# The opening of a windowed attention and SwiGLU kernel: one cast on another engine, gate matmuls among the attention's last products, the first projection begun on two chunks

## The chip, the cores and the metric

The kernel runs on one core of one Trainium2 chip. The metric is the device time of one launch in microseconds, taken as a median over runs. One execution was also taken by the hardware profiler; all starts and durations below come from it. The engines are called PE (TensorE), DVE (VectorE), ACT (ScalarE), POOL (GpSimd) and SP (SyncE). Each runs its own instructions in order, and they wait for each other by semaphores. Loads are issued from SP, ACT and POOL and are carried out by 16 DMA engines.

## The reference

There are 8 batches of 8 heads, 576 positions and 64 elements per head. Attention is causal with a window of 64 positions. The result, laid out as 4608 tokens by 512, goes through a gated block with 1536 hidden columns:

```
scores = (q @ k^T) / 8,  kept where 0 <= i - j < 64
attn   = exp(scores - max);  attn = attn / (sum(attn) + 1e-9)
x      = (attn @ v) as [4608, 512]
g      = x @ w_gate;  h = g * sigmoid(g) * (x @ w_val)
out    = h @ w_out
```

Inputs and output are float32. The kernel multiplies in bf16.

## The kernel before

**Tiles.** The 4608 tokens are nine tiles of 512. Tile t, up to the seventh, holds the first 512 positions of batch t; one later tile, called LAST, gathers the last 64 positions of all batches. The eight heads go in four pairs, u = 0 to 3. The model dimension has four chunks of 128 (one for each pair), the hidden dimension twelve blocks of 128.

**Stages of a tile.** `scores(t, u)` makes the products of one pair in a two-bank PSUM tile (tag "a", two buffers), and ACT takes their exponential into a tile E; from tile 1 on DVE multiplies by the mask. `totals` sums E by a matmul with ones; ACT takes the logarithm and then `invert` its negative exponential, so that r is the inverse sum. `mix` multiplies E by the values, and `scale` (DVE) multiplies by r and writes chunk u of xT. `values` is `mix` and then `scale`. `v2` is a copy of the values shifted by 64 rows, written by `shift_pair` on DVE. Then for each hidden block m, `gate_value(t, m)` runs four matmuls with wg and four with wv over the chunks of xT into two PSUM banks (tags "g" and "v" of pool `ps_f`, two buffers each); `gate_end` takes Silu on ACT and multiplies on DVE into block m of hT. `gate_part` does the matmuls of one chunk c for several blocks. Last, `project_part` multiplies hT with wo over the twelve blocks, into `ps_f` banks as well, and the output goes out through SP.

**Order.** The schedule is manual: each engine executes its instructions in the order in which the program writes them. In steady state, tile t's gate blocks are followed by tile t+1's scores and tile t's projection, interleaved by hand.

**The opening.** Tile 0's queries and keys come in float32 by SP and ACT queues, a pair at a time. `cast_first(u, i)` makes bf16 of them, with i = 0 for queries and 1 for keys. The table `casts` says on which engine. `turn_pe(u)` transposes both on PE, and ACT or DVE copies them out of PSUM. POOL then issues, on one queue, half of tile 0's values, the weights wg and wv in slices of columns, tile 1's raw keys `raw_k`, the last weight slice, tile 1's queries (`load_qk(1)`, four loads into q_s), and wo with tile 1's values among it:

```
    weights_gv(1280, 1536)
    load_qk(1)
    weights_o(0, 4)
    weights_o(4, 8)
    load_v(nc.gpsimd, v1[1], 1)
    weights_o(8, 12)
```

Loads issued by POOL use eight semaphores in turn, so each waits until the load eight places earlier has landed. `keep_warm` is a matmul into an unused bank.

During tile 0's gate blocks, ACT casts the raw keys of tile 1 in blocks 5 to 8 and PE transposes them in blocks 6 to 9. From block 9 on, `turn_q(1, u)` transposes tile 1's queries on DVE, one behind each block's hT. It needs all four loads of q_s. After block 11 come `scores(1, u)` and `columns(c0, c1)`, which is tile 0's projection for all four 128-row parts over blocks c0 to c1; the four banks it accumulates in are taken in the order g, v, g, v. They are the banks of gate blocks 10 and 11.

The lines of the profile that matter: L73 loads of q and k by runs, L87 q_s, L128 values, L166 wg and wv, L172 wo, L180 transposes on PE, L192 `turn_q`, L233 scores, L239 their exponential, L241 mask, L251 totals, L259 and L262 logarithm and inverse, L275 `mix`, L285 `scale`, L312 `gate_part`, L325 and L326 `gate_end`, L332 `gate_value`, L341 `project_part`, L450 casts.

Of the kernel before, what the change touches and what calls it, by code (L numbers as in the profile page):

```python
# [17 lines left out]
def kernel(  # L18
# [42 lines left out]
    def batch(t):  # L61
        return t if t < LAST else t - 1
# [51 lines left out]
    def load_qk(t):  # L114
        q_s = load_q(t)
        if t == 1:
            staged[t] = q_s, None
            return
        if t == LAST:
            groups = [(b, S - P) for b in range(4)]  # L120
        else:
            groups = [(batch(t), P * g) for g in range(4)]
        k_s = stage.tile([P, 4, 4, 4 * D], BF16, name="k_s", tag="k")
        staged[t] = q_s, load_k(k_s, groups)

    def load_v(eng, dst, t, which=range(4)):
        for i in which:
            eng.dma_start(  # L128
                dst[:, i], v[batch(t), :, P * i:P * i + P].rearrange("h r d -> r h d")
            )  # L130
# [19 lines left out]
    def shift_pair(t, u):  # L150
        hs = slice(2 * u, 2 * u + 2)
        a, b = v1[t % 2][:, :, hs], v2[t % 2][:, :, hs]
        nc.vector.tensor_copy(b[64:128, 1:4], a[64:128, 0:3])
        nc.vector.tensor_copy(b[0:64], a[0:64])
# [16 lines left out]
    def weights_o(c0, c1):  # L171
        nc.gpsimd.dma_start(  # L172
            wo[:, c0:c1, :],
            moe_w_out[P * c0:P * c1].rearrange("(c r) f -> r c f", r=P),
        )
# [73 lines left out]
    def totals(t, u, d_ps):  # L249
        for h in range(2):  # L250
            nc.tensor.matmul(  # L251
                d_ps[64 * h:64 * h + 64], ones[:, 0:D], weights[t, u][:, h, :]
            )

    def room(n):
        return fsb.tile([P, 2, 512], FP32, name="r", tag="r", bufs=4)[:, 0:n]

    def log(r, d_ps):
        nc.scalar.activation(r, d_ps, AF.Ln)  # L259

    def invert(r):
        nc.scalar.activation(r, r, AF.Exp, scale=-1.0)  # L262
# [8 lines left out]
    def mix(t, u, o_ps):  # L271
        E = weights.pop((t, u))
        for m in range(8):
            for h in range(2):
                nc.tensor.matmul(  # L275
                    blocks(o_ps[64 * h:64 * h + 64], t, m, m + 1),
                    (v1, v2)[m // 4][t % 2][:, m % 4, 2 * u + h, :] if t == LAST
                    else (v2, v1)[m % 2][t % 2][:, m // 2, 2 * u + h, :],
                    blocks(E[:, h, :], t, m, m + 1),
                )  # L280

    def scale(t, u, o_ps):
        if u == 0:
            xT[t] = att.tile([P, 4, 512], BF16, name="xT", tag="xT")
        nc.vector.tensor_mul(xT[t][:, u, :], o_ps, inverse.pop((t, u)))  # L285

    def values(t, u, o_ps):
        mix(t, u, o_ps)
        scale(t, u, o_ps)
# [12 lines left out]
    def mix_all(t):  # L302
        tiles = wide("ao_ps"), wide("ao_ps")
        for u in range(4):
            mix(t, u, tiles[u // 2][:, u % 2])
        for u in range(4):
            scale(t, u, tiles[u // 2][:, u % 2])

    def gate_part(t, ms, tiles, c):
        for m, pair in zip(ms, tiles):  # L310
            for ps, w in zip(pair, (wg, wv)):
                nc.tensor.matmul(  # L312
                    ps[:], w[:, c, P * m:P * m + P], xT[t][:, c, :],
                    start=(c == 0), stop=(c == 3),
                )

    def gate_tiles():
        return [ps_f.tile([P, 512], FP32, name=x + "_ps", tag=x) for x in "gv"]
# [19 lines left out]
    def project_part(t, ss, tiles, cs):  # L338
        for c in cs:
            for s, o_ps in zip(ss, tiles):  # L340
                nc.tensor.matmul(  # L341
                    o_ps[:], hT[t][:, c, P * s:P * s + P], wo[:, c, :],
                    start=(c == 0), stop=(c == 11),
                )
# [64 lines left out]
    def keep_warm(n):  # L409
        for _ in range(n):  # L410
            nc.tensor.matmul(warm[0:D], ones[:, 0:D], ones[:])
# [32 lines left out]
    on_v, on_p, on_a = nc.vector.tensor_copy, nc.gpsimd.tensor_copy, nc.scalar.copy  # L444
# [4 lines left out]
    def join(copy, dst, src):  # L449
        copy(dst.rearrange("r e (h d) -> r h e d", h=2), src)  # L450

    def one(name):
        return ps_a.tile([P, 2, 512], FP32, name=name, tag="a")[:, 0]

    casts = ((on_a, on_v), (on_p, on_a), (on_a, on_p), (on_v, on_a))

    def cast_first(u, i):
        join(casts[u][i], first[:, i, u], raw[i][:, 2 * u:2 * u + 2])

    def turn_pe(u):  # L460
        tps = [ps_f.tile([P, 512], BF16, name="tp", tag=x) for x in "gv"]
        for i in range(2):
            transposes(tps[i], first[:, i, u])
        (on_v if u else on_a)(queries[0][:, u, :], tps[0][:])
        split_k(kT[0][:, u, :], tps[1][:])
# [3 lines left out]
    turn_pe(0)  # L469
    cast_first(1, 0)  # L470
    cast_first(1, 1)
    load_v(nc.gpsimd, v1[0], 0, (2, 3))
    keep_warm(1)
    scores(0, 0)
    turn_pe(1)
    cast_first(2, 0)
    cast_first(2, 1)
    keep_warm(2)
    scores(0, 1)
# [12 lines left out]
        load_runs(nc.gpsimd, raw_k[:, hs], k, 1, hs)  # L492
    weights_gv(1280, 1536)
    load_qk(1)
    weights_o(0, 4)
    weights_o(4, 8)
    load_v(nc.gpsimd, v1[1], 1)
    weights_o(8, 12)
# [11 lines left out]
    def log_of(u):  # L510
        d_ps = one("d_ps")
        totals(0, u, d_ps)
        inverse[0, u] = room(1)[:, 0]
        log(inverse[0, u], d_ps)
# [6 lines left out]
        values(0, u, ps_f.tile([P, 512], FP32, name="ao_ps", tag="gv"[u])[:])  # L521
    for u in (2, 3):
        shift_pair(0, u)
    log_of(3)
    for u in (2, 3):
        invert(inverse[0, u])
    keep_warm(1)
    pairs = [gate_tiles() for _ in range(2)]
    for c in range(2):
        gate_part(0, (0, 1), pairs, c)  # L530
    for u in (2, 3):
        values(0, u, one("ao_ps"))
    for c in range(2, 4):
        gate_part(0, (0, 1), pairs, c)
    set_silu()
    for m in range(12):
# [11 lines left out]
        if 5 <= m < 9:  # L548
            u = m - 5
            join(on_a, keys[:, u], raw_k[:, 2 * u:2 * u + 2])  # L550
        if 6 <= m < 10:
            u = m - 6
# [10 lines left out]
    def columns(c0, c1):  # L563
        project_part(0, range(4), tiles, range(c0, c1))

    for u in range(4):
        scores(1, u)
        if u == 1:
            columns(0, 4)
    columns(4, 7)  # L570
    for u in (0, 2):
        d_ps, r = wide("d_ps"), room(2)
        for i in range(2):
# [5 lines left out]
    load_v(nc.gpsimd, v1[0], 2)  # L579
    for u in range(4):  # L580
        shift_pair(1, u)
    columns(7, 10)
    mix_all(1)
    columns(10, 12)
    for s in range(4):
# [75 lines left out]
```

## Time and profile before

| What | us |
|---|---|
| median of 6 runs (332.97 to 333.56) | 333.29 |
| the profiled execution's own time | 336.23 |
| its span, first to last instruction | 334.4 |
| PE busy | 321.9 (96%) |
| DVE busy | 210.9 (63%) |
| ACT busy | 168.7 (50%) |
| POOL busy | 139.3 (42%) |
| DMA, mean over the span | 130 GB/s |

The span is that of the profiled execution; 1.83 us of its own time lie around it. Busy shares are means over the span. The opening, tile 0 with tile 1's attention, ends at about 56 us. Inside it POOL's queue of loads is active all the time, and after it PE is busy for 272.2 of 278 us. A wait in the profile is idle time of an engine just before an instruction, with what released it. The granted clock of PE is full in every slice.

### The profile page before, as it was taken

How to read it: one execution, taken by the hardware profiler on the slowest of the kernel's cores; microseconds unless marked ns; L12 is line 12 of the kernel's file. 1: busy time of each engine (PE TensorE's matmuls, PEld its weight loads, DVE VectorE, ACT ScalarE, POOL GpSimd, SP SyncE). 2: the span in 40 equal slices, each digit the busy share in tenths (PEclk: the TensorE clock that was granted, in tenths of full speed). 3: DMA queues.
4: the chain of work that ended last, by engine and by line, in shares of the span. 5: the costliest groups of instructions: out<-in, count | busy, mean ns of one | idle time of the engine just before them, and what ended most of it. 6: DMA issues, size and time to landing. Idle time of an engine off the chain costs nothing.

```text
span 334.4 us, 6954 instructions
## 1 busy us (share of the span) xinstructions
PE 321.9 (96%) x2700; PEld 154.3 (46%) x2743; DVE 210.9 (63%) x325; ACT 168.7 (50%) x239; POOL 139.3 (42%) x249
## 2 busy tenths in 40 slices
PE   8899899999999999999999999999999999999995
PEld 4444344444544454445444544445444544454443
DVE  5855565587557756785669566956786576754431
ACT  5854547337533773367435653465348533853310
POOL 4944434865837993656123996164200000000000
PEclk9999999999999999999999999999999999999999
DMA  7999999999999969939941999199501320020013
GB/s 250 195 192 200 202 190 173 150 169 213 176 223 212 108 108 243 192 51 217 181 94 18 160 196 165 10 186 177 119 1 33 88 63 2 17 79 32 2 33 94
DMA packets 83249, 43.59 MB, mean 130 GB/s; under 512 B 63888, under 2 KB 77968, under 8 KB 83216
## 3 DMA queue, kind: packets, MB, share of 16 engines
q0 software_dynamic: 50416, 23.08, 56.2%
q1 hardware_dynamic: 31776, 19.02, 21.1%
q10 hardware_dynamic: 1024, 1.05, 1.1%
q8 instruction: 21, 0.34, 0.4%
q14 instruction: 12, 0.10, 0.1%
HBM read 54.00 MB, written 9.44 MB: 190 GB/s over the span
## 4 chain that ended last, share of the span: by engine, by line
PE 83%; DMA 12%; POOL 3%; issue 1%; SPq 0%; DVE 0%; POOLq 0%
PE o_ps L341 25%; PE g_ps L332 25%; PE v_ps L332 24%; DMA wo<-in_moe_w_out_dram 4%; DMA wv<-in_moe_w_val_dram 4%; DMA q_s<-in_q_dram 3%; PE s_ps L233 3%; PE ao_ps L275 2%; PE d_ps L251 2%; DMA q_f<-in_q_dram 1%; POOL wg L166 1%; POOL wv L166 1%; PE o_ps L377 1%; POOL v L128 1%; POOL qk_b L450 0%
## 5 line engine op out<-in xcount | busy, mean ns | idle before, releaser
L325 ACT ACTIVATE sg<-g_ps 128x512 f32<-128x512 f32 x108 | 64.4, 597 | 116.4 <-PE g_ps L332 87.7
L326 DVE TENSOR_TENSOR hT<-sg,v_ps 128x512 bf16<-128x512 f32 x108 | 74.7, 692 | 61.1 <-PE v_ps L332 49.8
L332 PE MATMUL g_ps<-xT,wg 128*128 128x512 bf16 x415 | 108.2, 379 | 0.9
L332 PE MATMUL v_ps<-xT,wv 128*128 128x512 bf16 x415 | 107.2, 379 | 0.1
L341 PE MATMUL o_ps<-wo,hT 128*128 128x512 bf16 x396 | 93.5, 380 | 1.8 <-DMA wo<-in_moe_w_out_dram 0.4
L107 POOL DMA_DIRECT2D k_s<-in_k_dram x112 | 60.4, 546 | 35.7 <-DMA q_s<-in_q_dram 21.3
L332 PEld LDWEIGHTS <-wv 128*128 128x128 bf16 x424 | 41.5, 98 | 50.0
L332 PEld LDWEIGHTS <-wg 128*128 128x128 bf16 x424 | 41.3, 98 | 49.5 <-issue 0.6
L341 PEld LDWEIGHTS <-hT 128*128 128x128 bf16 x420 | 39.0, 98 | 48.4 <-issue 4.0
L239 ACT ACTIVATE E<-s_ps 128x1024 bf16<-128x1024 f32 x36 | 35.2, 1020 | 9.3 <-PE s_ps L233 9.3
L202 DVE STREAM_TRANSPOSE kT<-k_s 128x512 bf16<-128x512 bf16 x28 | 35.9, 1281 | 0.0
L259 ACT ACTIVATE r<-d_ps 128x512 f32<-128x512 f32 (+1 forms) x33 | 20.8, 629 | 16.8 <-PE d_ps L251 16.7
L285 DVE TENSOR_TENSOR xT<-ao_ps,r 128x512 bf16<-128x512 f32 x36 | 22.4, 683 | 7.3 <-PE ao_ps L275 7.0
L241 DVE TENSOR_TENSOR E<-E,mask 128x1024 bf16<-128x1024 bf16 x28 | 19.5, 698 | 12.0 <-ACT E L239 12.0
L87 POOL DMA_DIRECT2D q_s<-in_q_dram x28 | 15.2, 553 | 23.2 <-DVE qT L192 13.3
L192 DVE STREAM_TRANSPOSE qT<-q_s 128x512 bf16<-128x512 bf16 x32 | 22.4, 703 | 2.3 <-DMA q_s<-in_q_dram 2.3
L262 ACT ACTIVATE r<-r 128x512 f32<-128x512 f32 (+1 forms) x33 | 22.0, 669 | 1.0
L148 POOL CAST v<-v_f 128x512 bf16<-128x512 f32 x20 | 11.9, 615 | 18.5 <-DMA v_f<-in_v_dram 13.1
L233 PE MATMUL s_ps<-qT,kT 64*64 64x128 bf16 (+1 forms) x640 | 12.4, 211 | 0.2
L387 ACT ACT_TABLE_LOAD x9 | 11.5, 1283 | 2.0 <-issue 1.9
L94 POOL DMA_DIRECT2D q_s<-in_q_dram x16 | 8.6, 629 | 9.2 <-DVE qT L192 9.2
L251 PE MATMUL d_ps<-E,ones 128*64 128x512 bf16 x72 | 11.4, 390 | 0.8 <-ACT E L239 0.8
(102 smaller groups left out, 185.8 us busy)
## 6 DMA issues: line engine op xcount, KB each, us to landing
q_s<-in_q_dram POOLq DMA_DIRECT2D x28, 248.0 KB, 6.8
k_s<-in_k_dram POOLq DMA_DIRECT2D x112, 56.0 KB, 4.9
v_f<-in_v_dram SPq DMA_DIRECT2D x22, 256.0 KB
v<-in_v_dram POOLq DMA_DIRECT2D x18, 128.0 KB, 4.9
wo<-in_moe_w_out_dram POOLq DMA_DIRECT2D x3, 512.0 KB, 12.6
v<-v SPq DMA_DIRECT2D x6, 256.0 KB
v<-v SPq DMA_DIRECT2D x6, 192.0 KB
q_f<-in_q_dram SPq DMA_DIRECT2D x4, 256.0 KB
```

The source lines that it names most:

```text
L107: nc.gpsimd.dma_start(k_s[p0:p0 + 32, g, :, 0:w], k[b, a:H:2, s:s + P].rearrange("u (r e) d -> r u (e d)", e=4) [:, :, 32 * c:32 * c + w],)
L192: nc.vector.transpose(queries[t][:, u, :].rearrange("r (e x) -> r e x", e=16), staged[t][0][:, u].rearrange("r (e d) -> r e d", d=D)[:, :, ...
L202: nc.vector.transpose(dst[:, u, :].rearrange("r (g x e) -> r g e x", g=4, e=4), k_s[:, :, u].rearrange("r g (e d) -> r g e d", d=D)[:, :, ...
L233: nc.tensor.matmul(blocks(s_ps[64 * c:64 * c + 64, h], t, lo, hi), zero[r] if src is None else src[r, u, x:x + 64], blocks(qT[r], t, lo, h ...
L239: nc.scalar.activation(E[:], s_ps[:], AF.Exp, scale=0.125)
L259: nc.scalar.activation(r, d_ps, AF.Ln)
L262: nc.scalar.activation(r, r, AF.Exp, scale=-1.0)
L285: nc.vector.tensor_mul(xT[t][:, u, :], o_ps, inverse.pop((t, u)))
L325: nc.scalar.activation(sg[:], g_ps[:], AF.Silu)
L326: nc.vector.tensor_mul(hT[t][:, m, :], sg[:], v_ps[:])
L332: nc.tensor.matmul(ps[:], w[:, c, P * m:P * m + P], xT[t][:, c, :], start=(c == 0), stop=(c == 3),)
L341: nc.tensor.matmul(o_ps[:], hT[t][:, c, P * s:P * s + P], wo[:, c, :], start=(c == 0), stop=(c == 11),)
```

## The change

Three edits, all in the opening, none in what is computed.

1. The cast of pair 2's queries moves from ACT to POOL and stands ahead of POOL's two value loads; the cast of pair 2's keys moves from POOL to ACT.
2. The gate matmuls of blocks 0 and 1 over chunks 0 and 1 are placed around the values of pairs 2 and 3: chunk 0, pair 2's values, chunk 1, pair 3's values, then chunks 2 and 3. The four gate banks are taken from the pool before `log_of(3)`, and one `keep_warm(1)` goes.
3. The first load of wo, of four blocks, becomes two loads of two blocks. Tile 0's projection begins with blocks 0 and 1, ahead of `scores(1, 0)`; the later groups of blocks are cut at 2, 5 and 8 instead of 4, 7 and 10 (the cut at 10 stays).

```diff
-    casts = ((on_a, on_v), (on_p, on_a), (on_a, on_p), (on_v, on_a))
+    casts = ((on_a, on_v), (on_p, on_a), (on_p, on_a), (on_v, on_a))
...
     cast_first(1, 1)
+    cast_first(2, 0)
     load_v(nc.gpsimd, v1[0], 0, (2, 3))
     keep_warm(1)
     scores(0, 0)
     turn_pe(1)
-    cast_first(2, 0)
     cast_first(2, 1)
...
     load_qk(1)
-    weights_o(0, 4)
+    weights_o(0, 2)
+    weights_o(2, 4)
     weights_o(4, 8)
...
+    pairs = [gate_tiles() for _ in range(2)]
     log_of(3)
     for u in (2, 3):
         invert(inverse[0, u])
-    keep_warm(1)
-    pairs = [gate_tiles() for _ in range(2)]
     for c in range(2):
         gate_part(0, (0, 1), pairs, c)
-    for u in (2, 3):
-        values(0, u, one("ao_ps"))
+        values(0, c + 2, one("ao_ps"))
     for c in range(2, 4):
         gate_part(0, (0, 1), pairs, c)
...
+    columns(0, 2)
     for u in range(4):
         scores(1, u)
         if u == 1:
-            columns(0, 4)
-    columns(4, 7)
+            columns(2, 5)
+    columns(5, 8)
...
     for u in range(4):
         shift_pair(1, u)
-    columns(7, 10)
+    columns(8, 10)
     mix_all(1)
     columns(10, 12)
```

## The prediction, made before the changed kernel had run

> **What bounds the kernel now.** I read the page's busy shares first: PE (TensorE) is busy 321.9 of 334.4 us. By stretches of time, 272.2 of 278 us are busy after 56 us, and about 49.7 of 56 before. So half of PE's idle time, some 6.3 us, lies in the opening, and only the opening is edited. Then the chain that ended last, in order of time (start, length, what):
>
> ```profile
> 8.57 0.83 POOL qk_b L450
> 9.40 0.65 POOL wg L166
> ...
> 15.81 12.10 DMA wv<-in_moe_w_val_dram
> ...
> 28.19 10.43 DMA q_s<-in_q_dram
> ```
> ```profile
> 38.62 12.57 DMA wo<-in_moe_w_out_dram
> 51.20 0.04 issue
> 51.24 1.89 PE o_ps L341 x8
> ```
>
> The reader is to see that from 15.81 to 51.24 us the chain holds no engine: one load follows another, and PE takes over at 51.24. These loads are the one GpSimd queue (q0). Each waits for the landing of the load eight places before it, so eight are under way at any time. By windows the DMA moves 201 GB/s from 19 to 28 us and 193 from 40 to 52. Third, what PE waited for in 0 to 56 us (total, times, longest), and the timeline where it waits:
>
> ```profile
> PE s_ps L233 <- DVE qT L192: 1.6, 2, 0.8
> PE g_ps L312 <- DVE xT L285: 0.6, 1, 0.6
> PE tp L180 <- POOL qk_b L450: 0.5, 1, 0.5
> PE o_ps L341 <- DMA wo<-in_moe_w_out_dram: 0.4, 1, 0.4
> PE tp L180 <- ACT k_b L450: 0.3, 1, 0.3
> ```
> ```profile
> 29.27 0.62 ACT L450 COPY k_b<-k_r 128x512 bf16<-128x512 bf16 x1 [1.58 <-DMA k_r<-in_k_dram]
> 39.67 0.71 DVE L192 STREAM_TRANSPOSE qT<-q_s 128x512 bf16<-128x512 bf16 x1 [2.30 <-DMA q_s<-in_q_dram]
> 40.30 0.65 DVE L326 TENSOR_TENSOR hT<-sg,v_ps 128x512 bf16<-128x512 f32 x1
> 41.49 0.65 DVE L326 TENSOR_TENSOR hT<-sg,v_ps 128x512 bf16<-128x512 f32 x1
> 51.24 1.89 PE L341 MATMUL o_ps<-wo,hT 128*128 128x512 bf16 x8 [0.39 <-DMA wo<-in_moe_w_out_dram]
> ```
>
> The first three waits are what the three edits remove. The last two, and DVE's wait for q_s at 39.67, are arrivals: landings set where PE stands at 29.95 (the transposes of the next keys, after ACT's cast at 29.27), at 40.4 and at 51.24.
>
> **What the Trainium skill says.** "DMA: Bandwidth & Descriptors", section on queues, rings and completion order, has each DMA engine take a ring's descriptors in order. The trace agrees: landings follow the issue order, about 1.3 us apart for 256 KB. "SBUF — State Buffer", section on the two separate sides, says that VectorE and GpSimd share a port pair under an exclusive lock. The trace fits: the GpSimd cast alone took 0.61 us, the one at 8.56 us, beside a VectorE cast, 0.845. "TensorE: Matmul & The Clock Gate", Part 1, says that an idle window of some 3.4 us lowers the clock. The trace grants 1.00 in every slice, and no wait I expect is over 1.3 us, so the dropped warming matmul costs no clock.
>
> **The change part by part.**
>
> *Casts of pair 2.* POOL now casts the queries (0.61 us, 0.845 as the upper bound) ahead of its two value loads, and ACT the keys (0.61) where it cast the queries; the two counts stay. ACT is in the same place (7.74 us). On PE the second four transposes lose their 0.46 us wait; VectorE's copy of the keys then follows its copy of the queries at 9.47 instead of 9.89, so scores of pair 2 and ACT's next exponentials come 0.4 earlier. On POOL's queue stand behind the cast the two value loads (1.87 us) and all weight loads. The cast can start at 6.70, if the third quarter of q is in. The trace doesn't show that landing: quarter 1 was in at 5.96, quarter 3 at about 8.4, and ACT took quarter 2 at 7.74 without a wait. Between, 6.8 is my estimate (256 KB at the window's 360 GB/s take 0.7 us); 7.74 is the late end. Then 6.85 + 0.61 + 1.87 = 9.3 against 9.36 for the first weight load: nothing. The late end gives 10.2 to 10.5, 0.9 to 1.1 us late; the early end 9.2, a gain of 0.2. The value loads go out 0.7 later (landing 12.4 and 13.4, after 11.7 and 12.7); shift_pair at 12.67, then values, can lose about 0.7, under the same cover as the next part.
>
> *Gate parts among sums and products.* Same instructions less one warming matmul (0.22 us). Now the eight matmuls of chunks 0 and 1 run around the values of pairs 2 and 3, so scaling pair 2 overlaps chunk 1. The last gate chunks began at 18.93 after a 0.60 us wait; with 0.4 from the casts, 0.22 from the warming matmul and 0.6 from the wait, PE is some 1.1 us ahead at 20 us (0.9 to 1.3; 0.3 if the values are late). What is late next: wv for columns 768 to 1279 lands at about 28.1 by POOL's waits, and block 6 needed it at 28.41. PE, 1.1 early, would wait 0.85 there. Then the key transposes, at 29.95 behind the landing of k_r, where PE waited 0.3 and now waits to the same 29.95. Gain kept: 0. If that cover were gone, it would be 1.1.
>
> *wo in two loads and two chunks first.* One more POOL issue (0.75 us, POOL idles between waits there), and every later load waits for a landing one place earlier; the last wo load is issued at 39.65 + instead of 38.62, but some 1.3 MB (three parts of wo and four of v) stand ahead of it in the queue, so its landing stays at 51.24. SP's queue carries nothing here that the change touches.
>
> columns(0, 2), eight matmuls of 0.22, move ahead of scores(1, 0), which PE could start at 40.43. They need four PSUM banks. Two of them are the value banks of blocks 10 and 11, which VectorE frees with hT at 40.30 + 0.65 = 40.95 and 41.49 + 0.65 = 42.14, behind the transposes that waited for q_s; the order of instructions shows both waits on DVE. They also need the first half of wo. The whole 512 KB was in by 41.98, so half is in at about 41.98 − 1.2 = 40.8. PE ends block 11 at 39.65, idles 1.15, runs three matmuls with a 0.1 wait, idles to 42.2: 2.55 − 0.65 = 1.9 us of idle time against 0.79 + 0.77 = 1.56 before. PE is thus 0.34 later when it has done chunks 0 to 7. Behind it stand scores, the exponentials on ACT, the masks on DVE and the totals: with matmuls at 0.225 the two later scores come at 46.6 (45.54 before), masks end at 49.8, totals run from 49.9. Chunk 8 could start at 50.85 + 0.34 = 51.2 while wo lands at 51.24: the old 0.39 wait becomes 0.05. The logarithms of pairs 2 and 3 end at 53.6 (52.5 before), the time at which mix_all wants their bank (53.66). Cost 0, or about 0.1 if these two margins miss.
>
> The sum: 0 (casts) + 0 (gate) + 0.1 (columns) = +0.1 us on the profiled execution's own 336.23 (334.4 span and 1.83 around it). That execution stands 2.94 above the median of 333.29; the difference carries over: 333.4.
>
> **The rivals.** A measurement of this kernel can tell about 0.2%, 0.67 us, from no change.
>
> *A, arrivals decide* (0.52): −0.3 to +0.5 us, as above. For it: three landings close the gain of each stage. Against it: margins of 0.05 us.
>
> *B, columns(0, 2) overshoots* (0.28, slower): PE stands in order behind a busy bank or the load. If the first half of wo completes no earlier than the whole did (41.98), idle time is 2.33 instead of 1.56 us, chunk 8 is ready at 51.6, 0.4 past the landing, and the logarithms are 0.8 later, so mix_all waits as much for its bank: +0.4 to +0.8 us. With the late end of the cast, all landings move 1 us too, up to +1.5. It decides from 0.39 us of added idle time. For it: two of four banks are proven late. Against it: half a load needs half the bytes.
>
> *C, the loads land earlier* (0.20, faster): from 14 to 19 us the DMA moved only 159 GB/s while POOL issued without a break, against 201 later; 5 us times 42 is 210 KB, 1.05 us at 201. If the new order around 7 to 9 us feeds the queue better, or the 0.2 us of an early cast is added, all landings come earlier and the 1.1 us of the gate parts can be kept: −0.4 to −1.1 us. For it: a later landing is all that holds PE. Against it: bytes and first weight issue are unchanged.
>
> **How the numbers follow.** The predicted time is A's, 333.4. A alone spans 333.0 to 333.8. To leave out no more than 2 in 10, the range takes C's and B's ends: 332.3 to 334.6. Faster by over 0.2% is most of C with a little of A, 0.21; slower most of B with a little of A, 0.29; within, 0.50.
>
> **What would show it.** Right: the key transposes near 29.95 with a PE wait for ACT of over 1 us before it (there or for wv), o_ps waiting for DVE hT for some 0.7 us near 42, and chunk 8 starting within 0.2 us of 51.24 on wo. Steps fail as follows. A first weight issue after 9.8 us makes the cast's cost real. Key transposes before 29.5 show that the loads moved, as C says. Chunk 8 behind PE's own work, without a wait for wo, is B. Work after 56 us changing by over 0.3 us would be outside all of these.

## The result, and the profile after

The changed kernel takes 334.71 us (median of 30 runs, 333.90 to 337.89) against 333.31 for the kernel before (65 runs). The ratio is 1.0047, interval [1.0037, 1.0057]: some 1.6 us slower by the ratio (the two medians differ by 1.40), where 333.4 and no change was the likeliest forecast, and just outside the range of 332.3 to 334.6.

The two profiled executions say the opposite: the changed kernel's own time was 335.50 (span 333.5), that of before 336.23 (span 334.4). None of the 65 runs of before reached 336.23; the highest was 335.11. So the first thing to read is a second execution of the kernel before (332.97 us, span 331.1). Timelines of POOL, of the first cast of tile 1's keys on ACT and of the first of its query transposes on DVE (start, length, engine, line, what; in brackets the idle time before and what ended it):

The kernel before, second execution:

```profile
5.52 0.61 POOL L450 CAST qk_b<-q_f 128x512 bf16<-128x512 f32 x1 [3.02 <-DMA q_f<-in_q_dram]
6.07 1.93 POOL L128 DMA_DIRECT2D v<-in_v_dram  x2
7.99 0.63 POOL L450 CAST qk_b<-k_f 128x512 bf16<-128x512 f32 x1
8.55 0.71 POOL L166 DMA_DIRECT2D wg<-in_moe_w_gate_dram  x1
...
27.98 0.62 ACT L450 COPY k_b<-k_r 128x512 bf16<-128x512 bf16 x1 [0.65 <-DMA k_r<-in_k_dram]
...
37.03 0.71 DVE L192 STREAM_TRANSPOSE qT<-q_s 128x512 bf16<-128x512 bf16 x1 [0.50 <-DMA q_s<-in_q_dram]
```

The first weight load goes out at 8.55 us, not at 9.36 as in the execution that the prediction was read from. In that one a quarter of q landed 0.57 us late and the cast on POOL took 0.845 us instead of 0.63. What waits for the loads starts 1.3 us earlier here at 27.98 and 2.6 us earlier at 37.03. The late issue goes with the first 1.3. The other 1.3 was lost between the two starts: they are 10.40 us apart in the first execution, and 8.92 to 9.40 in the twelve others with this order of loads; no run shows why. PE starts tile 1's first gate matmul at 52.95 instead of 56.12. PE's wait for wo, 0.39 us at 51.24, is not there at all: PE comes to chunk 8 behind its own work.

The chain that ended last is another one in this execution:

```profile
0.82 3.24 DMA q_f<-in_q_dram
...
20.49 1.02 PE g_ps L332 x4
```

Behind the first load of q it holds no load, and from 20.49 us to tile 1's first gate matmul nothing but PE. Of the three waits that the edits aimed at, PE has only that for xT (0.6 us); those for qT and for POOL's cast are absent. So two of the three waits were not there to be won in a usual execution.

The changed kernel, first execution, the chain that ended last:

```profile
6.81 0.61 POOL qk_b L450
7.42 1.87 POOL v L128 x2
9.29 0.70 POOL wg L166
...
16.46 12.77 DMA k_r<-in_k_dram
29.26 0.63 ACT k_b L450
...
40.02 0.66 DVE hT L326
40.72 1.24 PE o_ps L341 x5
...
48.53 0.57 PE d_ps L251 x4
49.12 1.03 ACT r L259
50.18 1.06 ACT r L262
51.24 0.92 ACT r L259
52.20 0.69 PE ao_ps L275 x32
```

The loads hold the chain only up to 29.26. From there it runs through three things that the change made: hT on DVE, which frees the bank that an early chunk needs; the totals; and the logarithms on ACT, for whose bank `mix_all` waits. No load of wo is in it. What PE waited for in 0 to 56 us (total, times, longest):

```profile
PE ao_ps L275 <- DVE v L154: 1.6, 3, 0.7
...
PE tp L180 <- ACT k_b L450: 0.4, 1, 0.4
PE o_ps L341 <- DVE hT L326: 0.4, 1, 0.4
...
PE ao_ps L275 <- ACT r L259: 0.2, 1, 0.2
```

The first line is the later value loads: the shift copies come late and `mix` waits. The waits that the change aimed at (s_ps for qT, g_ps for xT, tp for POOL's cast) are not in the list, though only the second of them was in a usual execution before, and these stand in their place. Tile 1's first gate matmul starts at 54.76, 1.81 after the usual 52.95.

Not all of the loss lies in the opening. From tile 1's first gate matmul to the end of the span the changed kernel takes 278.7 us, and 279.0 in a second execution (334.69 us, next to the median); in all twelve other executions, of before and of parts of the change, it is 278.1 to 278.3. The 0.5 and 0.7 us are lost at one place, the first totals of tile 3: counted from the same matmul, the projection behind them starts 60.47 and 60.66 us on, against 59.93 in before's second execution. The changed kernel, first execution, then the end of PE's wait in the second:

```profile
113.08 2.35 POOL L618 COPY maskl<-tri 128x64 bf16<-128x64 bf16 x8
113.38 1.45 DVE L241 TENSOR_TENSOR E<-E,mask 128x1024 bf16<-128x1024 bf16 x1 [0.23 <-ACT E L239]
...
114.89 0.41 PE L251 MATMUL d_ps<-E,ones 128*64 128x512 bf16 x2 [0.35 <-DVE E L241]
```
```profile
114.07 0.41 PE L251 MATMUL d_ps<-E,ones 128*64 128x512 bf16 x2 [0.54 <-DVE E L241]
```

The kernel before, second execution:

```profile
111.57 0.74 DVE L241 TENSOR_TENSOR E<-E,mask 128x1024 bf16<-128x1024 bf16 x1 [0.19 <-ACT E L239]
...
112.33 0.62 PE L251 MATMUL d_ps<-E,ones 128*64 128x512 bf16 x4
```

The mask multiplication of pair 1 takes 1.45 us (1.65 in the second execution) instead of 0.74, and both chains that ended last run through it. POOL's copies for the mask of LAST (L618) run beside it. They alone do not explain it: with edit 1 alone they start at 112.21, the multiplication at 112.53, and it takes 0.76. What makes it long, and in how many runs it is long, stays open.

### The profile page after: what moved, and what is told of

Same layout as the page of the kernel before. It is cut to its first block, busy times and chain, and to the rows that moved or that the text cites. A ratio compares the mean times of both kernels' runs of the same rounds, so it can differ in the third digit from the quotient of the medians.

```text
span 333.5 us, 6953 instructions
## 1 busy us (share of the span) xinstructions
PE 321.9 (97%) x2699; PEld 154.2 (46%) x2742; DVE 212.1 (64%) x325; ACT 168.7 (51%) x239; POOL 140.1 (42%) x250
## 4 chain that ended last, share of the span: by engine, by line
PE 86%; DMA 5%; POOL 3%; ACT 2%; DVE 1%; issue 1%; SPq 0%; DVEq 0%
PE g_ps L332 26%; PE o_ps L341 26%; PE v_ps L332 25%; DMA k_r<-in_k_dram 4%; PE s_ps L233 3%; PE d_ps L251 2%; PE ao_ps L275 2%; DMA q_f<-in_q_dram 1%; POOL wg L166 1%; POOL wv L166 1%; PE o_ps L377 1%; ACT r L259 1%; ACT E L239 1%; POOL v L128 1%; DVE E L241 0%
## 5 line engine op out<-in xcount | busy, mean ns | idle before, releaser
L241 DVE TENSOR_TENSOR E<-E,mask 128x1024 bf16<-128x1024 bf16 x28 | 20.4, 732 | 12.5 <-ACT E L239 12.5
L275 PEld LDWEIGHTS <-v 128*64 128x64 bf16 x576 | 10.8, 112 | 5.2 <-DVE v L154 2.6
L275 PE MATMUL ao_ps<-E,v 128*64 128x64 bf16 x576 | 11.4, 196 | 1.8 <-DVE v L154 1.6
```

Source lines behind the costliest of these rows:

```text
L275: nc.tensor.matmul(blocks(o_ps[64 * h:64 * h + 64], t, m, m + 1), (v1, v2)[m // 4][t % 2][:, m % 4, 2 * u + h, :] if t == LAST else (v2, v ...
```

## The experiments

All ratios are against runs of the kernel before on the same chip. "First weight issue" is POOL's first load of wg.

**The kernel before, once more.** No edit.

> The kernel before, profiled once more. If landings differ from one execution to the next (theory L), tile 1's first gate matmul, at 56.12 us in the first trace, comes earlier here, by 1 to 3 us, and so does the landing of the last wo load (51.24). If the first trace was typical (theory S), both stand within 0.3 us of these and the span is 334.4 within 0.4.

Measured: 332.97 us, first gate matmul of tile 1 at 52.95, 3.2 us earlier. The POOL issue that waits for the last load of wo starts at 48.08 instead of 51.48. Theory L holds: the first trace was of a late execution.

**Edit 1 alone.**

```diff
-    casts = ((on_a, on_v), (on_p, on_a), (on_a, on_p), (on_v, on_a))
+    casts = ((on_a, on_v), (on_p, on_a), (on_p, on_a), (on_v, on_a))
...
     cast_first(1, 1)
+    cast_first(2, 0)
     load_v(nc.gpsimd, v1[0], 0, (2, 3))
...
-    cast_first(2, 0)
     cast_first(2, 1)
```

> Edit 1 alone: pair 2's queries cast on POOL ahead of the value loads, its keys on ACT. Theory V (the later value loads cost: shift_pair and the values wait for them and nothing covers it): +0.7 to +1.4 us, with a PE wait for DVE's shift copies near 14 us. Theory P (the projection's two first chunks cost): 0, within 0.3. The forecast: 0, within 0.3.

Measured: 1.0031 [1.0017, 1.0044], +1.0 us. From POOL's timeline, and the cast on ACT that needs the keys:

```profile
6.57 0.62 POOL L450 CAST qk_b<-q_f 128x512 bf16<-128x512 f32 x1 [0.40 <-DMA q_f<-in_q_dram]
7.13 2.14 POOL L128 DMA_DIRECT2D v<-in_v_dram  x2
9.26 0.71 POOL L166 DMA_DIRECT2D wg<-in_moe_w_gate_dram  x1
...
28.71 0.62 ACT L450 COPY k_b<-k_r 128x512 bf16<-128x512 bf16 x1 [1.29 <-DMA k_r<-in_k_dram]
```

POOL waits 0.40 for the third quarter of q with the value loads and all weight loads behind it. The first weight issue moves from 8.55 to 9.26, k_r's cast from 27.98 to 28.71. The chain that ended last goes on from k_r to the first load of wo, which POOL issues once k_r has landed:

```profile
16.50 12.18 DMA k_r<-in_k_dram
...
28.97 11.11 DMA wo<-in_moe_w_out_dram
```

PE begins tile 0's projection at 40.12 behind that landing, instead of at 39.36. Theory V's signs are there too, +1.0 us and PE waits of 0.35 and 0.30 for the shift copies near 14 us. But these waits were covered: PE begins block 2 at 20.58, and at the same 20.58 in the run below that has the casts behind the value loads.

**Edit 2 alone.** The gate parts interleaved, one `keep_warm(1)` fewer, as in the diff of the change.

> Edit 2 alone: gate matmuls of chunks 0 and 1 around the values of pairs 2 and 3, one warming matmul fewer. Forecast: 0, since PE waits for the landing of k_r at 29.95 anyway. If landings do not bind in a usual execution: -0.6 to -0.9 us. Theory V and P: no loss here, 0 or a gain.

Measured: 1.0014 [1.0000, 1.0029]; medians 333.32 and 333.13. No gain, as forecast, and perhaps a loss of up to 1 us. PE is 0.3 us ahead at the key transposes (28.82 against 29.12) and loses it where scores of pair 1 wait 0.45 us for qT, transposed behind the landing of q_s.

**Edit 3 alone.** The split load, the early chunks and the new cuts, as in the diff of the change.

> Edit 3 alone: first wo load in two, columns(0, 2) ahead of scores(1, 0). Theory P: +0.8 to +1.6 us, PE waiting for DVE hT on the value bank of block 11 ahead of the scores. Theory V: 0, within 0.3. Forecast: 0 to +0.1.

Measured: 1.0027 [1.0019, 1.0035], +0.9 us. The two places, from PE's timeline:

```profile
39.89 1.24 PE L341 MATMUL o_ps<-wo,hT 128*128 128x512 bf16 x5 [0.20 <-DVE hT L326]
...
51.37 0.69 PE L275 MATMUL ao_ps<-E,v 128*64 128x64 bf16 x32 [0.23 <-ACT r L259]
```

Three matmuls of the early chunks run, then PE waits for the bank of block 11; later the second half of `mix_all` waits for the bank of the logarithms.

**Pair 2's casts swapped, but behind the value loads.**

```diff
-    casts = ((on_a, on_v), (on_p, on_a), (on_a, on_p), (on_v, on_a))
+    casts = ((on_a, on_v), (on_p, on_a), (on_p, on_a), (on_v, on_a))
```

> Pair 2's queries on POOL and keys on ACT, as in edit 1, but the cast stands behind POOL's two value loads, where the keys' cast stood. Theory Q (place in the queue: in edit 1 POOL waits for the third quarter of q ahead of the value loads, so the first weight load goes out 0.7 us later and every landing with it): 0 within 0.3 us, first weight issue as before near 8.55. Theory E (which engine casts what is the cost): +0.7 to +1.2 us as with edit 1 alone.

Measured: 1.0004 [0.9995, 1.0013], first weight issue at 8.57. Which engine casts what costs nothing that the times show (−0.2 to +0.4 us); the place in POOL's queue costs the 1.0 us.

**One more cast on POOL ahead of the weights.**

```diff
+    join(on_p, keys[:, 0], raw[1][:, 4:6])
     weights_gv(0, 256, 0, 2)
```

> The kernel before with one more cast of pair 2's keys on POOL into an unused tile, between POOL's cast and its first weight load; nothing else moves, the value loads stay in time. Theory T (the queue has a threshold: a first weight issue up to about 8.9 us is covered by loads under way, a later one delays every landing): issue near 9.1 to 9.2, k_r's landing 0.3 to 0.8 us later than 28.0, +0.4 to +1.0 us in time. Rival V (in edit 1 the later value loads were the cost, not the weight issue): 0, within 0.2.

Measured: 1.0037 [1.0022, 1.0053], +1.2 us. POOL, ACT and PE:

```profile
8.58 0.89 POOL L450 CAST k_b<-k_f 128x512 bf16<-128x512 f32 x1
9.42 0.70 POOL L166 DMA_DIRECT2D wg<-in_moe_w_gate_dram  x1
...
29.58 0.62 ACT L450 COPY k_b<-k_r 128x512 bf16<-128x512 bf16 x1 [2.55 <-DMA k_r<-in_k_dram]
...
30.25 0.40 PE L180 MATMUL tp<-identb,k_b 128*128 128x128 bf16 x4 [1.02 <-ACT k_b L450]
```

The value loads go out where they always did (6.11 us), so a late weight issue is enough for a cost of this size, and rival V falls. It was 0.87 us late, and k_r 1.6 us, beyond the expected 0.8.

**Edit 2, with pair 2's keys cast on DVE.**

```diff
-    casts = ((on_a, on_v), (on_p, on_a), (on_a, on_p), (on_v, on_a))
+    casts = ((on_a, on_v), (on_p, on_a), (on_a, on_v), (on_v, on_a))
```

> Edit 2 alone and, instead of edit 1, pair 2's keys cast on DVE, so that no cast stands between POOL's value loads and its weight loads. Theory Q: the first weight issue comes 0.5 us earlier than 8.55, landings 0.5 earlier, and the lead that edit 2 gives PE is kept: -0.4 to -0.9 us. Rival (landings have their own pace and do not follow the first issue): 0 to +0.2, as with edit 2 alone.

Measured: 0.9992 [0.9985, 0.9999], −0.3 us; medians 332.88 and 333.20. The first weight issue came at 8.03, and yet k_r was cast at 28.13 and q_s transposed at 37.21, no earlier than before. Theory Q fails in this direction: an earlier issue buys no earlier landing. The time lies between theory Q and the rival. This is the one version that beats both kernels, by less than the 0.2% at which the prediction counted a difference.

**Edit 3 with the old cuts.**

```diff
+    columns(0, 2)
     for u in range(4):
         scores(1, u)
         if u == 1:
-            columns(0, 4)
+            columns(2, 4)
     columns(4, 7)
```

(with the split load)

> Edit 3 with the old cuts: columns(0, 2), scores 0 and 1, columns(2, 4), scores 2 and 3, columns(4, 7), totals, columns(7, 10). Theory M (two waits: about 0.33 us on the value bank of block 11, and about 0.4 where mix_all waits for the bank of the late logarithms because a whole block more stands before scores(1, 2)): only the first is left, +0.3 to +0.5 us. Theory F (the early chunks alone cost, or the split load does): +0.8 to +1.0 as with edit 3.

Measured: 1.0007 [0.9996, 1.0019], about +0.2 us, not told apart from nothing. PE waited 0.60 us for hT, having come earlier, and nowhere for a logarithm.

**The new cuts alone.**

```diff
     for u in range(4):
         scores(1, u)
         if u == 1:
-            columns(0, 4)
-    columns(4, 7)
+            columns(0, 5)
+    columns(5, 8)
...
-    columns(7, 10)
+    columns(8, 10)
```

> Only the later cuts of edit 3: scores 0 and 1, columns(0, 5), scores 2 and 3, columns(5, 8), totals, columns(8, 10). No early chunks, no split load. Theory M: scores(1, 2) come 0.9 us later and columns(7, 8) no longer stand behind the totals, so mix_all waits for the bank of the late logarithms: +0.3 to +0.6 us, with a PE wait for ACT's logarithm, and no wait on hT. Rival (the wait on hT is all of edit 3's cost): 0, within 0.2.

Measured: 0.9999 [0.9989, 1.0009]. The wait for the logarithm is in the trace, 0.23 us before 50.97, but the times show no loss. Theory M's number missed.

**Edits 2 and 3.** The change without edit 1.

> The changed kernel without edit 1. If the costs add up (edit 1 about 1.0 us by itself, edit 3 about 0.9, edit 2 none): +0.6 to +1.0 us against before, the first weight issue back near 8.6. If the edits hide each other, as in the changed kernel's first trace where edit 3 filled the wait for q_s: +1.2 to +1.6, no better than the full change.

Measured: 1.0013 [1.0004, 1.0023], +0.4 us, first weight issue at 8.56. Less than edit 3 alone, though the intervals touch.

**The changed kernel once more.**

> The changed kernel once more. Theory L (landings differ between executions, and the first trace of before was a late one): the first weight issue stays at 9.2 to 9.4 us, as in its first trace, because the queue's order sets it; k_r lands at 28.9 to 29.3; tile 1's first gate matmul within 0.4 us of 54.5, 1.5 us behind the 52.95 of the usual execution of before; +1.2 to +1.8 us in time.

Measured: 1.0068 [1.0044, 1.0093] on four runs. The first weight issue came at 9.04, k_r was cast at 28.27 and tile 1's first gate matmul started at 53.75, all earlier than expected: POOL did not wait for the third quarter of q this time. The starts fit the table below. The time does not follow from them: tile 1's first gate matmul is 0.80 behind the usual 52.95, and the rest is what tile 3 loses.

**Tile 1's query loads ahead of the last weight slice.** On top of edit 2 and the keys' cast on DVE:

```diff
-    weights_gv(1280, 1536)
     load_qk(1)
+    weights_gv(1280, 1536)
```

> Edit 2, pair 2's keys cast on DVE, and tile 1's four query loads issued ahead of the last slice of wg and wv. If q_s sets where edit 2's lead is lost: q_s lands near 34.5, DVE's transposes no longer hold hT of blocks 10 and 11, scores(1, 1) start without a wait: -0.4 to -0.8 us. Rival (the last weight slice becomes late for block 10, or the last wo load near 48 binds): -0.2 to +0.3.

Measured: 1.0007 [0.9999, 1.0016]. The rival holds: block 10 now waits 0.6 us for wg and 0.3 for wv.

**All traces side by side.** Windows of 14 to 19 us give the DMA rate; the other columns are starts in the timelines.

| Execution | first weight issue, us | DMA 14 to 19 us, GB/s | k_r cast on ACT, us |
|---|---|---|---|
| edit 2, keys on DVE | 8.03 | 196 | 28.13 |
| q loads earlier | 8.26 | 196 | 27.86 |
| before, second | 8.55 | 195 | 27.98 |
| edits 2 and 3 | 8.56 | 195 | 27.98 |
| cuts alone | 8.56 | 192 | 27.98 |
| casts behind values | 8.57 | 196 | 28.03 |
| edit 2 | 8.60 | 195 | 28.11 |
| edit 3, old cuts | 8.60 | 194 | 27.95 |
| edit 3 | 8.86 | 196 | 28.13 |
| changed, second | 9.04 | 178 | 28.27 |
| edit 1 | 9.26 | 154 | 28.71 |
| changed, first | 9.28 | 161 | 29.26 |
| before, first | 9.36 | 159 | 29.27 |
| extra cast | 9.42 | 140 | 29.58 |

Up to 8.9 us the landing stands at 28.0, within 0.15. Beyond, counted from 8.55 and 27.98, it moves by 0.6 to 1.8 times as much as the issue, and most of the loss lies in the stretch from 14 to 19 us: for the first execution of before 195 − 159 = 36 GB/s over 5 us is 180 KB, 0.9 of its 1.3 us at 200 GB/s. From 19 to 28 us all fourteen run at 200 to 203. The 159 GB/s that the prediction took for a trait of the kernel was the mark of a late execution.

## Why the prediction was wrong, point by point

**The base.** The step that failed first is "the difference carries over". The profiled execution was 2.94 us above the median, the prediction said so, and it took every margin from that execution all the same. Up to k_r its loads were late in the way that edit 1 makes them late: issue at 9.36 there, 9.28 in the changed kernel. With it came two waits that a usual execution does not have, and the view that landings set where PE stands at 29.95, at 40.4 and at 51.24: in the usual execution the chain has no landing at these places.

**Casts of pair 2.** "9.3 against 9.36 for the first weight load: nothing." The 9.3 was right (9.28 and 9.04 measured, the wait for the third quarter included); the 9.36 should have been 8.55. The term is +0.5 to +0.7 us of issue instead of 0, and it costs 1.0 us alone ([0.6, 1.5] from its ratio). The sign set for a costly cast, an issue after 9.8 us, was too late for the same reason. Swapping the casts behind the value loads costs nothing. The later value loads were covered in edit 1 alone, but not in the whole change: block 2 begins at 20.21 and 20.69 in its two executions, and at 20.01 with edits 2 and 3. That POOL held the loads was the right mechanism, and the size was off because the base was.

**Gate parts.** The lead of 1.1 us, 0.4 of it from the casts, was too large: edit 2 alone is 0.3 us ahead at the key transposes. That none of it is kept was right. The cover was named at k_r; in the execution of edit 2 alone it is the landing of q_s, one step later.

**Columns.** The bank wait behind hT was predicted and is there: 0.44 us recorded in the first trace of the changed kernel, with the start at 40.72, against the predicted 42.2. So was the half load of wo in time. The term that failed is "the old 0.39 wait becomes 0.05": usually PE has no wait for wo to give up, so lost time counts from the first tenth. The second margin, 53.6 against 53.66 for the bank of the logarithms, was missed: PE waits there in every trace with the new cuts. Edit 3 costs +0.9 us alone against the predicted 0 to 0.1; rival B put this at +0.4 to +0.8, and at up to 1.5 with a late cast. The change ended there, in part by luck: the half load was not late, and what tile 3 loses was in no rival.

**The sum.** Alone the edits cost 1.0, 0.5 (from none to 1.0) and 0.9 us, and together 1.6: they do not simply add up. Edits 2 and 3 give +0.4 us, which leaves 1.1 for edit 1 on top of them, but not all of it is the late loads. In the changed kernel's second execution tile 1's first gate matmul starts at 53.75, no later than with edits 2 and 3 (53.87), and some 0.7 us are lost in tile 3. In the first it starts at 54.76, and tile 3 loses 0.5. The prediction had no term for tile 3: it took the work behind the opening as unchanged, and named a change of over 0.3 us there as outside all its theories. Every part of the change that was run leaves that work unchanged; the whole does not.

**What stays open.** The times do not split edit 3. Old cuts cost 0.07% [−0.04, 0.19] and cuts alone −0.01% [−0.11, 0.09], the two together 0.27%. A reading that fits is that the bank wait makes the scores late and the cuts then take away the work that would have covered the logarithms; no run separates it from the spread. Also open is why the mask multiplication of tile 3 is long in the whole change only, and what slows the loads between 14 and 19 us after a late issue: the table shows that it happens, not by what.

## What to carry to other kernels

Before margins of tenths are read from a trace, its own time has to stand near the median; when it does not, look for the landing that came late in it, since a wait seen there may be absent in most runs. An instruction that waits for a load should not stand ahead of the issue of other loads on the same queue: the cast ahead of POOL's two value loads cost 1.0 us, and the same cast behind them, ahead of the weight loads but with its input landed, nothing. Filling a wait with other work pays only if that work's buffers are free and no later cover is used up. And the whole change has to be followed to the end of its trace: here a part of the loss lay in tile 3, some 60 us behind the opening, and no part of the change showed it alone.

## What was not expected of the hardware

The landing of a long queue of loads did not follow its start evenly. An issue 0.5 us earlier than usual (8.03) brought nothing, one 0.87 later (9.42) cost 1.6 us at k_r. And a single POOL cast of 128 × 512 took 0.61 to 0.89 us in these traces, the long ones at 8.56 (0.845) and 8.58 us (0.89). A mask multiplication on DVE beside POOL's copies took 1.45 and 1.65 us in the two executions of the changed kernel and 0.76 with edit 1 alone.
